# The second feed-forward's output product in seven-product block form, turned, in a written order

## The chip, the cores and the metric

The kernel runs on one core of a Trainium2 chip. Its engines run at the same time, each through its own queue in order: TensorE (PE, with its weight loads PEld), VectorE (DVE), ScalarE (ACT), GpSimd (POOL) and SyncE (SP), which issues nearly all DMAs. The metric is the device time of one execution in microseconds (us). Three runs of the kernel before took 812.83, 813.78 and 814.72 us; the median is 813.78.

## The reference

Three stages, all in float32:

```python
def _attn_ref(q, k, v):                        # q, k, v: 4 batches, 8 heads, 576 rows, 64 columns
    scores = scale * np.matmul(q, k.transpose(0, 1, 3, 2))
    ...                                        # heads 0-3: a local mask, heads 4-7: every 32nd row
    return np.matmul(softmax(scores), v)

def _moe_ref(x, w_gate, w_val, w_out):         # x: 2304 tokens x 512; inner width 1536
    g = x @ w_gate
    silu = g * (1.0 / (1.0 + np.exp(-g)))
    return silu * (x @ w_val) @ w_out

def _moe2_ref(x, w1, w2, w3, w_out):           # inner width 768
    h = np.maximum(np.maximum(x @ w1, x @ w2), x @ w3)
    return h @ w_out                           # 2304 x 512
```

The change concerns the last line, `h @ w_out`.

## The kernel before

Matrix products keep float32 accuracy by splitting each operand into a high part, rounded to the matmul's type, and a low part, the rest. A product is then three matmuls: high x high, high x low, low x high (`product`, L643; `factor_product`, L770). Making the two parts is one ScalarE copy and one subtraction on VectorE or GpSimd (`split`, L169).

**The first half**, up to 530.7 us, does attention and the first feed-forward. The tokens run in five columns ("chunks") of up to 448 tokens; for each chunk and each of 12 slices f of the inner width a slot holds gate, value and output products (`emit_gate`, `emit_val`, `emit_out`). Beside it the weights of the second feed-forward are made ready in the order of the list `later` and stored to DRAM (`pair_steps` L256 for w1 to w3, `wo2_steps` L291 for w_out). The result y, transposed (512 rows x 2304 tokens), is stored to `ydr`. A scheduler orders most of this from estimated times; only the beginning is written out by hand.

**The second half** runs in three passes of 768 tokens, each as two column blocks of `TB` = 384. Its first part, the three products y @ w1, w2, w3, is done in blocks of two by two with seven block products in place of eight (the Strassen-Winograd form). Per pass there are three pairs g of inner slices and in each three matrices i, nine groups, 27 in all. `Group` (L780) computes one: with A for the weight's factors and B for y's, seven products of two row halves x three terms = 6 matmuls of 384 columns each, 42 in all, in three PSUM banks a, b, c. `head` has A11 (B11) into a and A12 (B21) into b; `middle` S2 (T2) into a, S1 (T1) into c, S3 (T3) into a; `tail` A22 (T4) into a and S4 (B22) into c. Between products into bank a ScalarE takes snapshots (`snap`, L787) that VectorE adds in later (`emit`, L795). The maximum over the three matrices is kept in t11, t12, t21, t22; at i = 2 it is split into h's high and low parts. The tail of a group is issued behind the head of the next.

The weights' seven factors, high and low, come in one DMA of 1792 KB per group into a ring of `NRING` = 4 tiles (`load_w`, L763). y's blocks are loaded into raw tiles, the factors T1 to T4 are made from them, and all are split (`load_y` L734, `split_y` L754).

**The output product before** (`mm` L841, `out2` L853): for each block of 128 tokens j, six inner slices x three terms = 18 matmuls with h as the stationary operand and 512 columns of w_out moving, into a bank z; 18 blocks in three passes, 324 matmuls. w_out is loaded once, 3072 KB. The first inner slices of blocks 0 and 1 (`z_early`) are free to move ahead, and the scheduler puts them between groups. Each z is copied to `osb` by VectorE or ScalarE and stored; the last one in two halves, on two queues.

## Time and profile before

| | before |
|---|---|
| median of 3 runs | 813.78 us (812.83 to 814.72) |
| profiled execution | 814.75 us, of which the span is 813.0 us |
| TensorE busy | 795.3 us, 98% of the span, 4588 matmuls |
| VectorE, ScalarE, GpSimd busy | 542.8, 384.2, 235.6 us |
| granted TensorE clock, mean | 0.996 |
| DMA | 200.50 MB, 247 GB/s |
| second half | from 530.70 us |

The span goes from the first to the last instruction on the core; the profiled execution's time is 1.75 us longer. Matmuls overlap in the pipeline and the busy time contains each one's whole latency, so a busy share says how seldom TensorE had nothing, and not at what pace it worked: the pace is the distance between starts.

### The profile page before, as it was taken

How to read it: one execution, taken by the hardware profiler on the slowest of the kernel's cores; microseconds unless marked ns; L12 is line 12 of the kernel's file. 1: busy time of each engine (PE TensorE's matmuls, PEld its weight loads, DVE VectorE, ACT ScalarE, POOL GpSimd, SP SyncE). 2: the span in 40 equal slices, each digit the busy share in tenths (PEclk: the TensorE clock that was granted, in tenths of full speed). 3: DMA queues.
4: the chain of work that ended last, by engine and by line, in shares of the span. 5: the costliest groups of instructions: out<-in, count | busy, mean ns of one | idle time of the engine just before them, and what ended most of it. 6: DMA issues, size and time to landing. Idle time of an engine off the chain costs nothing.

```text
span 813.0 us, 12942 instructions
## 1 busy us (share of the span) xinstructions
PE 795.3 (98%) x4588; PEld 711.5 (88%) x4588; DVE 542.8 (67%) x1104; ACT 384.2 (47%) x856; POOL 235.6 (29%) x237
## 2 busy tenths in 40 slices
PE   6999999999999999999999999999999999999998
PEld 5777777888998998888999999999999989989986
DVE  5899997888969899799993863634454344613440
ACT  6999994455454634555342543423242123512220
POOL 2534442022312432314232664502212121402110
PEclk9899999999999999999999999999999999999999
DMA  9998887777766887757676997789646566634402
GB/s 281 322 326 290 303 311 270 262 242 226 261 235 208 264 285 246 264 208 258 231 262 212 346 392 294 281 342 354 237 181 232 168 210 213 260 148 181 181 1 77
DMA packets 69688, 200.50 MB, mean 247 GB/s; under 512 B 8088, under 2 KB 33432, under 8 KB 66040
## 3 DMA queue, kind: packets, MB, share of 16 engines
q1 hardware_dynamic: 69480, 199.55, 70.0%
q8 instruction: 36, 0.59, 0.3%
q14 instruction: 28, 0.23, 0.1%
q10 hardware_dynamic: 144, 0.13, 0.0%
HBM read 157.97 MB, written 41.68 MB: 246 GB/s over the span
## 4 chain that ended last, share of the span: by engine, by line
PE 55%; DVE 4%; DMA 2%; issue 1%; ACT 1%; SPq 0%; POOL 0%; DVEq 0%; ACTq 0%
PE ps_a L775 13%; PE ps_z L849 9%; PE ps_c L775 7%; PE ps_b L775 3%; PE ps_y L645 3%; PE ps_y L647 3%; PE ps_y L646 3%; PE ps_v L645 3%; PE ps_v L647 3%; PE ps_v L646 2%; PE ps_g L645 2%; PE ps_g L646 2%; PE ps_g L647 2%; DMA wr<-wsdr 1%; DVE pr L552 1%
## 5 line engine op out<-in xcount | busy, mean ns | idle before, releaser
L680 POOL TENSOR_TENSOR hl<-ht,hh 128x448 fp32r<-128x448 f32 x48 | 61.6, 1284 | 228.1 <-ACT hh L676 206.4
L176 POOL TENSOR_TENSOR hl<-t,hh 128x384 fp32r<-128x384 f32 x36 | 37.7, 1050 | 208.0 <-ACT hh L173 160.0
L775 PE MATMUL ps_a<-yhT,wr 128*128 128x384 f32 x324 | 94.6, 339 | 1.1 <-ACT s L789 1.1
L645 PE MATMUL ps_g<-xh,wh_g 128*128 128x448 f32 (+1 forms) x240 | 90.8, 378 | 1.0 <-ACT ht L664 1.0
L645 PE MATMUL ps_v<-xh,w_v 128*128 128x448 f32 (+1 forms) x240 | 91.2, 380 | 0.4 <-DVE ht L671 0.2
L646 PE MATMUL ps_g<-xl,wh_g 128*128 128x448 f32 (+1 forms) x240 | 89.8, 374 | 0.0
L647 PE MATMUL ps_y<-hh,w_o 128*128 128x448 f32 (+1 forms) x240 | 89.4, 373 | 0.3 <-DVE w_o L249 0.3
L647 PE MATMUL ps_g<-xh,wl_g 128*128 128x448 f32 (+1 forms) x240 | 89.5, 373 | 0.0
L646 PE MATMUL ps_y<-hl,w_o 128*128 128x448 f32 (+1 forms) x240 | 89.2, 372 | 0.0
L646 PE MATMUL ps_v<-xl,w_v 128*128 128x448 f32 (+1 forms) x240 | 89.2, 372 | 0.0
L647 PE MATMUL ps_v<-xh,w_v 128*128 128x448 f32 (+1 forms) x240 | 89.1, 371 | 0.0
L789 ACT ACTIVATE s<-ps_a 128x384 f32<-128x384 f32 x81 | 39.4, 490 | 99.0 <-PE ps_a L775 98.7
L676 ACT ACTIVATE hh<-ht 128x448 fp32r<-128x448 f32 (+1 forms) x60 | 35.3, 588 | 104.7 <-DVE ht L671 93.4
L645 PE MATMUL ps_y<-hh,w_o 128*128 128x448 f32 (+1 forms) x240 | 84.3, 380 | 0.0
L849 PE MATMUL ps_z<-wo2t,hh 128*128 128x512 f32 x216 | 64.8, 392 | 0.9 <-ACT osb L867 0.7
L775 PEld LDWEIGHTS ps_a<-yhT,wr 128*128 128x128 f32 x324 | 59.7, 188 | 2.6 <-ACT s L789 2.1
L775 PE MATMUL ps_a<-ylT,wr 128*128 128x384 f32 x162 | 54.8, 338 | 0.0
L645 PEld LDWEIGHTS ps_g<-xh,wh_g 128*128 128x128 f32 x240 | 45.4, 189 | 7.1 <-ACT ht L664 1.8
L645 PEld LDWEIGHTS ps_v<-xh,w_v 128*128 128x128 f32 x240 | 45.1, 188 | 6.5 <-DVE ht L671 1.1
L647 PEld LDWEIGHTS ps_g<-xh,wl_g 128*128 128x128 f32 x240 | 45.3, 189 | 5.4 <-DVE wl_g L249 0.4
L647 PEld LDWEIGHTS ps_y<-hh,w_o 128*128 128x128 f32 x240 | 45.1, 188 | 5.6 <-DVE w_o L249 0.7
L645 PEld LDWEIGHTS ps_y<-hh,w_o 128*128 128x128 f32 x240 | 45.0, 188 | 5.6
(150 smaller groups left out, 1843.2 us busy)
## 6 DMA issues: line engine op xcount, KB each, us to landing
wr<-wsdr SPq DMA_DIRECT2D x27, 1792.0 KB, 7.3
raw<-in_w_dram SPq DMA_DIRECT2D x60, 512.0 KB, 6.0
w_v<-wvdr SPq DMA_DIRECT2D x48, 512.0 KB, 4.5
w_o<-wodr SPq DMA_DIRECT2D x48, 512.0 KB, 4.6
wsdr<-whi SPq DMA_DIRECT2D x27, 256.0 KB, 2.9
wvdr<-w_v SPq DMA_DIRECT2D x12, 512.0 KB, 3.7
wodr<-w_o SPq DMA_DIRECT2D x12, 512.0 KB, 3.9
wsdr<-w SPq DMA_DIRECT2D x18, 256.0 KB, 3.3
```

The costliest lines, as they stand in the source:

```text
L176: return a.ins, lo_eng.tensor_tensor(lo, src, f32(hi), ALU.subtract).ins
L552: eng.tensor_tensor(pv, self.k[:, 0:i + 1, :], self.q[:, r:r + 1, :].to_broadcast([128, i + 1, D]), ALU.mult)
L645: nc.tensor.matmul(ps, wh, xh, start=first, stop=False)
L646: nc.tensor.matmul(ps, wh, xl, start=False, stop=False)
L647: nc.tensor.matmul(ps, wl, xh, start=False, stop=last)
L676: return nc.scalar.activation(hs[c, f][0], t, AF.Copy).ins
L680: return eng.tensor_tensor(hl, t, f32(hh), ALU.subtract).ins
L775: nc.tensor.matmul(ps, wts[:, c, a, ks], y[k][b], start=first and k == q == 0, stop=k == 1 and q == 2, skip_group_check=True,)
L789: nc.scalar.activation(s, self.a, AF.Copy)
L849: nc.tensor.matmul(z[j], a[:, ts], w[:, f, b], start=f == q == 0, stop=f == NF2 - 1 and q == 2)
```

## The change

The output product gets the seven-product form too, and is turned: w_out's factors are the stationary operand (from the same ring, as a fourth matrix i = 3 of each pair g, made by `pair_steps(3, g)`), h's factors move, 384 tokens at a time, and the result is stored transposed; the host turns it back. So h is no longer split block by block: for each pair g the blocks t11 to t22 become factors (`Factors.combine`) and then high and low parts (`Factors.split`), three subtractions on VectorE and one on GpSimd, seven copies on ScalarE, five low parts on VectorE and two on GpSimd (T3, B22). The same class serves y, whose blocks B11, B21, B22 are loaded straight into the tiles that later hold their low parts. The conversion steps wait in a list, `waiting`, and `some(n)` issues the next n of them at written places. `outputs` runs one pass's output: for each half m of 128 rows seven products of 18/2 = 9 matmuls (three pairs x three terms); the parts of A11, A12 and S1 that need only pairs 0 and 1 come first, around the last group's tail. The next y is loaded and converted inside `outputs`. The ring has five tiles; the three weights of an output hold three of them until the pass ends. From the eleventh slot of the last chunk to the end, `manual_schedule` keeps the written order.

The change in the diff, cut to its core:

```diff
-NRING = 4
+NRING = 5
...
+            if i == 3:
+                a12, a21 = a21, a12
...
+        eng = nc.vector if (c, f) == (NC - 1, NF - 1) else nc.gpsimd
+        last_val[:] = [m, high_h(c, f, t), low_h(c, f, t, eng)]
 
...
+    class Factors:
+
+
+        def __init__(self, p, tag):
+            self.p, self.tag, self.parts, self.raw = p, tag, {}, {}
+
+        def part(self, q, f):
+            return self.p.tile([128, TB], F32R, name=f"{self.tag}{q}{f}", tag=f"{self.tag}{q}{f}")
+
+        def fresh(self, f):
+            r = self.raw[f] = r_p.tile([128, TB], F32, name=f"r{f}", tag=f, bufs=3 if f == "T3" else 1)
+            return r
+
+        def combine(self):
+            b12 = self.raw["T3"]
+            nc.vector.tensor_tensor(self.fresh("T1"), b12, self.raw["B11"], ALU.subtract)
+            nc.gpsimd.tensor_tensor(b12, self.raw["B22"], b12, ALU.subtract)
+            nc.vector.tensor_tensor(self.fresh("T2"), self.raw["B22"], self.raw["T1"], ALU.subtract)
+            nc.vector.tensor_tensor(self.fresh("T4"), self.raw["B21"], self.raw["T2"], ALU.subtract)
+
+        def split(self, f):
+            src = self.raw.pop(f)
+            hi, lo = self.part("h", f), self.parts.get(f) or self.part("l", f)
+            self.parts[f] = hi, lo
+            split(hi, lo, src, nc.scalar, nc.gpsimd if f in ("T3", "B22") else nc.vector)
+
+    waiting = []
+
+    def some(n):
+        for _ in range(min(n, len(waiting))):
+            waiting.pop(0)()
+
+    def conversion(fs, names):
+        return [fs.combine] + [lambda f=f: fs.split(f) for f in names]
+
+    def load_y(p):
+        y = [Factors(y_p, f"y{k}") for k in range(2)]
+        for k in range(2):
+            for n in ("B11", "B12", "B22", "B21"):
+                if n == "B12":
+                    r = y[k].fresh("T3")
+                else:
+                    y[k].parts[n] = y[k].part("l", n)
+                    r = y[k].raw[n] = f32(y[k].parts[n])
+                m, t = 2 * int(n[1]) - 2 + k, (2 * PASSES[p] + int(n[2]) - 1) * TB
+                for c, i0, i1, o in pieces(t // STRIDE, (t + TB) // STRIDE):
+                    nc.sync.dma_start(
+                        r[:, o * STRIDE:(o + i1 - i0) * STRIDE], ydr[c][:, m, i0 * STRIDE:i1 * STRIDE]
+                    )
+        for k in range(2):
+            waiting.extend(conversion(y[k], FACTORS[:-1]))
+        waiting.extend(lambda k=k: y[k].split("B22") for k in range(2))
         return y
 
     ring = {}
...
+    def factor_product(ps, pieces, piece, wts, bs, first, last):
+        c = pieces.index(piece)
+        for n, ((w, ks), (bh, bl)) in enumerate(zip(wts, bs)):
+            for q, (a, b) in enumerate(((0, bh), (0, bl), (1, bh))):
                 nc.tensor.matmul(
-                    ps, wts[:, c, a, ks], y[k][b], start=first and k == q == 0, stop=k == 1 and q == 2,
-                    skip_group_check=True,
+                    ps, w[:, c, a, ks], b, start=first and n == q == 0,
+                    stop=last and n == len(wts) - 1 and q == 2, skip_group_check=True,
                 )
+
+    def banks(first=None):
+        ps = (first or m_p, m_p, m_p)
+        return (q.tile([128, 512], F32, name=f"ps_{n}", tag=n)[:, :TB] for q, n in zip(ps, "abc"))
+
+    def snap(ps, n):
+        s = s2_p.tile([128, TB], F32, name=f"s{n}", tag=f"s{n}", bufs=1 + (n < 3))
+        nc.scalar.activation(s, ps, AF.Copy)
+        return s
 
...
-            t = run[blk]
+            t = to = run[blk]
+            if self.i == 2:
+                h2.setdefault(self.g, Factors(h2_p, f"h{self.g}"))
+                to = h2[self.g].fresh("T3") if blk == "12" else t
+                h2[self.g].raw.setdefault("B" + blk, t)
             if s is None:
-                nc.vector.tensor_tensor(t, ps, t, ALU.max)
+                nc.vector.tensor_tensor(to, ps, t, ALU.max)
             else:
                 nc.vector.tensor_tensor(s, ps, s, ALU.add)
-                nc.vector.tensor_tensor(t, s, t, ALU.max)
-            if self.i == 2:
-                f, h = 2 * self.g + int(blk[0]) - 1, int(blk[1]) - 1
-                hh, hl = h2[f]
-                ts = slice(h * TB, (h + 1) * TB)
-                split(hh[:, ts], hl[:, ts], t, nc.scalar, nc.gpsimd)
+                nc.vector.tensor_tensor(to, s, t, ALU.max)
 
...
+        def finish(self):
+            if self.i == 2:
+                waiting.extend(conversion(h2[self.g], FACTORS))
+
     run, h2 = {}, {}
...
+    class Out:
+
+
+        def __init__(self, p, m):
+            self.p, self.m = p, m
+            self.w = [ring[p, g, 3] for g in range(NFP)]
+            self.a, self.b, self.c = banks()
+
+        def mul(self, n, piece, f, gs=range(NFP), last=False):
+            ms = slice(self.m * 128, (self.m + 1) * 128)
+            factor_product(
+                getattr(self, n), OUT_PIECES, piece, [(self.w[g], ms) for g in gs], [h2[g].parts[f] for g in gs],
+                gs[0] == 0 and piece in ("A11", "A12", "S1"), last
+            )
+
+        def snap(self, n):
+            setattr(self, f"s{n}", snap(self.a, n))
+
+        def emit(self, blk, ps, s=None):
+            t0 = (2 * PASSES[self.p] + int(blk[1]) - 1) * TB
+            rows = slice((int(blk[0]) - 1) * 256 + self.m * 128, (int(blk[0]) - 1) * 256 + (self.m + 1) * 128)
+            osb = osb_p.tile([128, TB], F32, name="osb", tag="osb")
+            if s is None:
+                nc.scalar.activation(osb, ps, AF.Copy)
             else:
-                nc.scalar.activation(osb, z[j], AF.Copy)
-            nc.sync.dma_start(out[t0:t0 + 128, :], osb)
-
-        for j in range(2 * TB // 128):
-            mm(j, z_late if j < 2 else range(NF2))
-            done(j)
-        z.clear()
-
+                nc.vector.tensor_tensor(osb, ps, s, ALU.add)
+            nc.sync.dma_start(out[rows, t0:t0 + TB], osb)
+
+    def outputs(p, grp, y):
+        early = range(NFP - 1)
+        final = [NFP - 1]
+        o = [Out(p, m) for m in range(2)]
+        o[0].mul("a", "A11", "B11", early)
+        grp.tail()
+        o[0].mul("b", "A12", "B21", early)
+        o[0].mul("c", "S1", "T1", early)
+        o[1].mul("a", "A11", "B11", early)
+        o[1].mul("b", "A12", "B21", early)
+        o[1].mul("c", "S1", "T1", early)
+        grp.finish()
+        ends = p == NP - 1
+        some(len(waiting))
+        if not ends:
+            y = load_y(p + 1)
+            load_w(*work[len(ring)])
+        for t in o:
+            t.mul("a", "A11", "B11", final)
+            t.snap(1)
+            t.mul("b", "A12", "B21", final, True)
+            t.emit("11", t.b, t.s1)
+        some(4)
+        for t in o:
+            t.mul("a", "S2", "T2")
+            t.snap(2)
+            some(1)
+        for t in o:
+            t.mul("c", "S1", "T1", final)
+            t.mul("a", "S3", "T3")
+            t.snap(3)
+            t.emit("22", t.c, t.s3)
+            some(2)
+        for t in o:
+            some(2)
+            if ends and t is o[1]:
+                t.mul("c", "S4", "B22", last=True)
+                t.emit("12", t.c, t.s2)
+                t.mul("a", "A22", "T4", last=True)
+                t.emit("21", t.a)
+            else:
+                t.mul("a", "A22", "T4", last=True)
+                t.emit("21", t.a)
+                t.mul("c", "S4", "B22", last=True)
+                t.emit("12", t.c, t.s2)
+        for _ in range(NFP):
+            if len(ring) < len(work):
+                load_w(*work[len(ring)])
+        return y
 
     wdr = {(n, f): dram.tile([128, 2, 512], F32, name=f"w{n}dr{f}") for n in "vo" for f in range(NF)}
-    wsdr = {(i, g): dram.tile([128, 7 * 2 * 256], F32, name=f"wsdr{i}{g}") for i in range(3) for g in range(NFP)}
-    wo2dr = dram.tile([128, NF2, 2, 512], F32, name="wo2dr")
+    wsdr = {(i, g): dram.tile([128, 7 * 2 * 256], F32, name=f"wsdr{i}{g}") for i in range(4) for g in range(NFP)}
 
     first = [("g", 0), ("v", 0)]
     for f in range(NF):
@@ -943,12 +1005,16 @@
             for i, st in enumerate(attention_steps(c)):
                 fill.setdefault((c - 1) * NF + i - 3, []).extend(st)
         later = [step for g in range(NFP) for i in range(3) for step in pair_steps(i, g)]
-        later += [step for f in range(NF2) for step in wo2_steps(f)]
+        later += [step for g in range(NFP) for step in pair_steps(3, g)]
         due, done = 0.0, 0
+        seam = ExitStack()
         for s, (c, f) in enumerate(slots):
+            if (c, f) == (NC - 1, SEAM + 1):
+                seam.enter_context(tc.manual_schedule())
             if c > 0:
-                reload("v", f)
-                reload("o", f)
+                if c < NC - 1 or f <= SEAM:
+                    reload("v", f)
+                    reload("o", f)
                 emit_val(c, f, emit_gate(c, f))
             with ExitStack() as tied:
                 if c == 0:
@@ -967,15 +1033,19 @@
                 assert not later
...
+                y = load_y(0)
                 load_w(0, 0, 0)
+            if c == NC - 1:
+                some(len(waiting) if f == NF - 1 else 5)
             if c > 0:
                 emit_out(*pending)
                 pending = c, f
+        seam.close()
         emit_out(*pending)
     one.close()
 
...
-            if (g, i) == (NFP - 1, 2):
-                mm(0, z_early)
-                grp.tail()
-                mm(1, z_early)
-                before = None
-                out2(p)
-                if p + 1 < NP:
-                    y = [split_y(raw[k]) for k in range(2)]
-
+        for p in range(NP):
+            h2.clear()
+            for g in range(NFP):
+                for i in range(3):
+                    grp = Group(p, g, i, y)
+                    grp.head()
+                    some(2)
+                    if before is not None:
+                        before.tail()
+                    grp.middle()
+                    if before is not None:
+                        before.finish()
+                    some(4)
...
+                    before = grp
+            y = outputs(p, grp, y)
+            before = None
 
...
-    return r.results[0]["out_0_dram"]
+    return _np.ascontiguousarray(r.results[0]["out_0_dram"].T)
```

Three places of the order in which the instructions stand. In the names, `y0hB11` is the high part of factor B11 of y's first row half, `h2lT2` the low part of T2 of h's pair 2; `ps_a`, `ps_b`, `ps_c` are the PSUM banks, `wr` a ring tile.

TensorE, last group of the kernel, from its product S3 to its product A22, before:

```order
L775 MATMUL ps_a_8038<-yhT3_7536,wr_7853 128x384
L775 MATMUL ps_a_8038<-ylT3_7537,wr_7853 128x384
L775 MATMUL ps_a_8038<-yhT3_7536,wr_7853 128x384
L775 MATMUL ps_a_8038<-yhT4_7512,wr_7853 128x384
L775 MATMUL ps_a_8038<-ylT4_7513,wr_7853 128x384
L775 MATMUL ps_a_8038<-yhT4_7512,wr_7853 128x384
```

and now:

```order
L790 MATMUL ps_a_8345<-y1hT3_7763,wr_8126 128x384
L790 MATMUL ps_a_8403<-h0hB11_8037,wr_8186 128x384
L790 MATMUL ps_a_8403<-h0lB11_8038,wr_8186 128x384
L790 MATMUL ps_a_8403<-h0hB11_8037,wr_8186 128x384
L790 MATMUL ps_a_8403<-h1hB11_8254,wr_8266 128x384
L790 MATMUL ps_a_8403<-h1lB11_8255,wr_8266 128x384
L790 MATMUL ps_a_8403<-h1hB11_8254,wr_8266 128x384
L790 MATMUL ps_a_8345<-y0hT4_7697,wr_8126 128x384
```

Before, A22 followed S3 on the same bank at once; now the output's first product, of six matmuls into another bank, stands between them.

SyncE's queue, before, where the second pass's y is loaded, in the middle of the first pass (L742 y, L766 weights):

```order
L766 DMA wr_6062<-wsdr21_138 128x3584
L742 DMA rB11_6064<-ydr3_105 128x384
L742 DMA rB12_6066<-ydr4_106 128x384
L742 DMA rB21_6068<-ydr3_105 128x384
L742 DMA rB22_6070<-ydr4_106 128x384
L742 DMA rB11_6079<-ydr3_105 128x384
L742 DMA rB12_6081<-ydr4_106 128x384
L742 DMA rB21_6083<-ydr3_105 128x384
L742 DMA rB22_6085<-ydr4_106 128x384
L766 DMA wr_6156<-wsdr02_133 128x3584
L766 DMA wr_6220<-wsdr12_136 128x3584
```

and now, at the first pass's end (L770 y, L783 weights, L887 results):

```order
L783 DMA wr_6525<-wsdr32_142 128x3584
L783 DMA wr_6585<-wsdr00_131 128x3584
L770 DMA y0lB11_6680<-ydr3_105 128x384
L770 DMA rT3_6682<-ydr4_106 128x384
L770 DMA y0lB22_6684<-ydr4_106 128x384
L770 DMA y0lB21_6686<-ydr3_105 128x384
L770 DMA y1lB11_6688<-ydr3_105 128x384
L770 DMA rT3_6690<-ydr4_106 128x384
L770 DMA y1lB22_6692<-ydr4_106 128x384
L770 DMA y1lB21_6694<-ydr3_105 128x384
L783 DMA wr_6696<-wsdr10_134 128x3584
L887 DMA out_0_dram<-osb_6706 128x384
```

The eight loads of y moved from the first pass's groups to its output, into tiles that the groups read until then, and stand behind the load of the next pass's first weights and ahead of its second and of all results.

VectorE, behind the last group of the kernel, before (the last maxima, then copies of z):

```order
L806 TENSOR_TENSOR t21_8004<-ps_a_8038,t21_8004 128x384
L808 TENSOR_TENSOR s2_8080<-ps_c_8040,s2_8080 128x384
L809 TENSOR_TENSOR t12_8012<-s2_8080,t12_8012 128x384
L865 COPY osb_8160<-ps_z_8132 128x512
L865 COPY osb_8204<-ps_z_8185 128x512
L859 COPY osb_8248<-ps_z_8229 128x256
```

and now:

```order
L832 TENSOR_TENSOR s2_8385<-ps_c_8347,s2_8385 128x384
L833 TENSOR_TENSOR rT3_8428<-s2_8385,t12_8309 128x384
L739 TENSOR_TENSOR rT1_8461<-rT3_8428,t11_8205 128x384
L741 TENSOR_TENSOR rT2_8464<-t22_8245,rT1_8461 128x384
L742 TENSOR_TENSOR rT4_8466<-t21_8301,rT2_8464 128x384
L176 TENSOR_TENSOR h2lB11_8469<-t11_8205,h2hB11_8468 128x384
L176 TENSOR_TENSOR h2lB21_8473<-t21_8301,h2hB21_8472 128x384
L176 TENSOR_TENSOR h2lT2_8477<-rT2_8464,h2hT2_8476 128x384
L176 TENSOR_TENSOR h2lT1_8481<-rT1_8461,h2hT1_8480 128x384
L176 TENSOR_TENSOR h2lT4_8489<-rT4_8466,h2hT4_8488 128x384
L886 TENSOR_TENSOR osb_8504<-ps_b_8404,s1_8499 128x384
```

Behind the last maximum (`rT3`, L833) three combinations and five low parts now stand on VectorE ahead of the first result.

## Rows read from the trace of the kernel before

**Rows 1.** Windows: length, busy us (instructions) by engine, clock, DMA share, GB/s.

```profile
430.00:530.70 100.70, 100.70 (x498) 92.99 (x497) 54.68 (x79) 42.96 (x84) 51.25 (x46) 1.00 0.85 305
530.70:813.00 282.30, 275.87 (x1459) 259.72 (x1458) 114.42 (x195) 80.00 (x165) 50.96 (x48) 1.00 0.54 197
```

**Rows 2.** Windows of TensorE: line 775 (groups), then line 849 (output).

```profile
530.70:813.00 282.30, 206.94 (x1134) 1.00 0.54 197
530.70:813.00 282.30, 81.30 (x324) 1.00 0.54 197
```

**Rows 3.** Chain of waits, pieces in order of time: start us, us, what.

```profile
530.70 1.28 PE ps_a L775 x6
...
552.02 2.12 PE ps_a L775 x12
...
792.72 16.64 PE ps_z L849 x72
```

**Rows 4.** Waits of TensorE, 500 to 813 us: total us, times, longest.

```profile
PE ps_a L775 <- ACT s L789: 1.1, 2, 0.6
PE ps_z L849 <- ACT osb L867: 0.7, 1, 0.7
PE ps_b L775 <- DMA wr<-wsdr: 0.7, 1, 0.7
```

**Rows 5.** Timeline near the end: start us, us, engine, instruction, [idle before, releaser].

```profile
786.50 0.33 PE L775 MATMUL ps_a<-yhT,wr 128*128 128x384 f32 x1
786.93 0.49 ACT L789 ACTIVATE s<-ps_a 128x384 f32<-128x384 f32 x1 [1.95 <-PE ps_a L775]
...
787.47 0.44 PE L775 MATMUL ps_a<-yhT,wr 128*128 128x384 f32 x1 [0.64 <-ACT s L789]
```

**Rows 6.** VectorE by line and shape, 530 to 813 us: count, busy us, mean ns.

```profile
L809 DVE TENSOR_TENSOR t<-s,t 128x384 f32<-128x384 f32 x54 | 36.0, 667 | 1.5
L808 DVE TENSOR_TENSOR s<-ps_c,s 128x384 f32<-128x384 f32 x36 | 20.0, 556 | 41.7 <-ACT s L789 33.2 <-PE ps_c L775 8.4
...
L176 DVE TENSOR_TENSOR ylB<-rB,yhB 128x384 fp32r<-128x384 f32 x12 | 7.5, 630 | 4.1 <-ACT yhB L173 4.1
...
L751 DVE TENSOR_TENSOR rT<-rB,rT 128x384 f32<-128x384 f32 x4 | 3.6, 904 | 0.1
```

**Rows 7.** ScalarE and GpSimd by line and shape, the same stretch.

```profile
L789 ACT ACTIVATE s<-ps_a 128x384 f32<-128x384 f32 x81 | 39.4, 490 | 99.0 <-PE ps_a L775 98.7
L173 ACT ACTIVATE hh<-t 128x384 fp32r<-128x384 f32 x36 | 18.9, 524 | 38.3 <-DVE t L809 27.2 <-DVE t L806 11.0
...
L176 POOL TENSOR_TENSOR hl<-t,hh 128x384 fp32r<-128x384 f32 x36 | 37.7, 1050 | 208.0 <-ACT hh L173 160.0 <-issue 21.5 <-PE ps_a L775 19.3
```

**Rows 8.** Timeline of VectorE and GpSimd while y's factors are made.

```profile
649.93 0.56 DVE L750 TENSOR_TENSOR rT<-rB,rT 128x384 f32<-128x384 f32 x1 [0.59 <-DMA rB<-ydr]
...
650.00 1.36 POOL L748 TENSOR_TENSOR rB<-rB,rB 128x384 f32<-128x384 f32 x1 [1.24 <-DMA rB<-ydr]
...
650.52 1.25 DVE L751 TENSOR_TENSOR rT<-rB,rT 128x384 f32<-128x384 f32 x1
```

**Rows 9.** DMA issues, 500 to 813 us: count, KB each, median us to landing.

```profile
wr<-wsdr SPq DMA_DIRECT2D x26, 1792.0 KB, 7.3
out_dram<-osb SPq DMA_DIRECT2D x17, 256.0 KB, 2.0
...
rB<-ydr SPq DMA_DIRECT2D x12, 192.0 KB, 7.7
...
out_dram<-osb ACTq DMA_DIRECT2D x1, 128.0 KB, 1.8
```

**Rows 10.** Timeline of the end.

```profile
808.96 0.39 PE L849 MATMUL ps_z<-wo2t,hl 128*128 128x512 f32 x1
...
810.25 0.37 ACTq L862 DMA_DIRECT2D out_dram<-osb  x1
```

**Rows 11.** Timeline of TensorE where the second half begins.

```profile
530.34 0.37 PE L647 MATMUL ps_y<-hh,w_o 128*128 128x448 f32 x1
530.68 0.44 PE L775 MATMUL ps_a<-yhB,wr 128*128 128x384 f32 x1
```

More of the change, by code (lines that the diff above doesn't have):

```diff
@@ L784, in __init__ @@
             self.g, self.i, self.w, self.y = g, i, ring[p, g, i], y
[L785 to L790 removed]
+            self.a, self.b, self.c = banks(a_p if (p, g, i) == (0, 0, 0) else m_p)
         def mul(self, ps, piece, f, first, last):
[L793 removed]
+            halves = [(self.w, slice(k * 128, (k + 1) * 128)) for k in range(2)]
+            factor_product(ps, PIECES, piece, halves, [t.parts[f] for t in self.y], first, last)
         def emit(self, blk, ps, s=None):
             if self.i == 0:
[L798 removed]
+                t = run[blk] = t_p.tile([128, TB], F32, name=f"t{blk}", tag=f"t{blk}", bufs=1 + (blk in ("11", "22")))
                 if s is None:
@@ L993, in tile_attention_swiglu_maxout @@
-        wo2 = wo2_p.tile([128, NF2, 2, 512], F32R, name="wo2t")
+        a_p = sub(two, "a", 1, space=PS, reuse_waits="tile")
+        work = []
+        for p in range(NP):
+            work += [(p, g, i) for g in range(NFP) for i in range(3)] + [(p, g, 3) for g in range(NFP)]
         for n in range(1, NRING):
-            last = load_w(*work[n])
-        with tc.issue_after(last):
-            nc.sync.dma_start(f32(wo2), wo2dr)
+            load_w(*work[n])
+        ctx.enter_context(tc.manual_schedule())
```

121 lines of the change are left out of this document (17 added, 104 removed).

## The prediction

> **What bounds the kernel now.** I read four views of the second half, from 530.70 us to the end. First, the windows by stage: TensorE is busy 275.87 of 282.30 us at the full granted clock, VectorE 114.42, ScalarE 80.00, GpSimd 50.96, DMA 0.54 of its engines [rows 1]. Nothing but TensorE is near its limit, and in the last 100 us of the first half the other engines have 46 us or more to spare as well. Second, the same window for the two matmul lines alone gives the counts: 1134 products of 384 columns in the groups, 324 of 512 columns in the output [rows 2]. Third, the chain of waits runs through those products, and its pieces give the pace without the overlap that the busy time contains: twelve of 384 columns take 2.12 us, so 0.1765 us each, and 72 of 512 columns take 16.64 us, so 0.2311 us each [rows 3]. Fourth, the waits of TensorE name what little is lost: 1.1 us for ScalarE's snapshots, 0.7 for an output bank, 0.7 for a weight load [rows 4].
>
> From these the half adds up. 1134 x 0.1765 + 324 x 0.2311 = 200.2 + 74.9 = 275.1 us of work. TensorE's first product starts at 530.70 and its last, at 808.96, ends 0.23 later [rows 3, 10], which is 278.5 us: 3.4 us are idle, of which rows 4 name 2.5 and the pipeline's refill after each stop the rest.
>
> **What the change does, part by part.** *The output product.* 324 products of 512 columns go. Seven products, each two row halves x three pairs x three terms, make 126 per pass and 378 in three passes, all of 384 columns: the group's own shape, with the same one weight load for each. 378 x 0.1765 = 66.7 us against 74.9: **-8.2 us**, all on TensorE, which is the path.
>
> *The old idle time.* The stop of 0.6 us stands where S3 and A22, both into bank a, follow each other: A22 needs the snapshot between them [rows 4, 5]. In the new order a full product stands there at least; the first order piece shows it. The output bank's stop goes because the output has six banks of its own sequence. The weight stop at the start of the second pass goes because the two weights that begin a pass have slots while the output still holds three of five. **-3.4 us**; bounds 0 and -3.4; I take all of it and count what comes in its place.
>
> *Waits that can come.* After a product's last slot ends ScalarE starts 0.25 us later (786.50 + 0.18 to 786.93) and TensorE 0.05 us after ScalarE ends [rows 5]; two VectorE instructions in a row are 0.04 apart (649.93 + 0.56 to 650.52) [rows 8].
> (a) Between S2 and S3 stands S1 alone, 1.06 us, for a chain of 0.25 + 0.49 + 0.05 = 0.79 us [rows 5, 7]. The margin is 0.27 us, 27 times. Bounds 0 and 2.7 (0.1 each); I take 0.2.
> (b) The end of a pass, three times. The last pair's factors start when S4 ends; 30 products of the output that use pairs 0 and 1 cover 30 x 0.1765 = 5.3 us. The chain on VectorE (third order piece) is add 0.56, max 0.67, T1 0.56, T2 0.56, T4, low half of B11 0.63 [rows 6, 8], with 0.25 + 6 x 0.04 + 0.05 of hand-overs. T4 falls beside GpSimd's T3. Row 650.52 has just that pair: T4 took 1.25 us beside GpSimd's 1.36 [rows 8], against 0.904 in the mean [rows 6]. With 1.25 the chain is 4.8 us, without any conflict 4.0, and with B11's low half at 1.25 as well 5.4. Bounds 0 and 0.3 in all; I take 0.
> (c) After pairs 0 and 1, six times. ScalarE's queue has the high half of T2 ahead of the next group's first snapshot, and behind that snapshot stands S2. From the end of S3: 0.25 + 0.49 (snapshot), 0.56 (emit), 0.56 (T1), 0.56 (T2), 0.52 (high half), 0.49 (snapshot) [rows 6 to 8], with hand-overs 3.7 us, against four products of six, 4.24 us. T2 at 1.25 makes it 4.35, T1 too 5.04. Bounds 0 and 4.8 us (6 x 0.8); I take 0.4.
> (d) The next y, twice. Sixteen conversion steps of VectorE now lie inside the output: 2 x (0.56 + 0.56 + 1.25 + 5 x 0.63) = 11.0 us, four emits 2.2, hand-overs 0.8: 14.0 us. They start at 11.4 us after the last group's S3 (48 matmuls 8.5, twelve more 2.1, then 0.25 and the emit's 0.56) and TensorE asks for the second half's T2 at 26.5 (the tail's 12 matmuls, the output's 126, and 12 of the next group): 15.1 us. Two low halves of T3 on GpSimd may block 0.7 us each. Bounds 0 and 0.8; I take 0.2.
> (e) The y loads themselves. They go into tiles that the products just left, so B22's load waits for S4, 3.2 us after S3. A load of 192 KB took 7.7 us to land [rows 9], so 10.9; the first combine comes at 11.4. But the loads queue behind one of 1792 KB (7.3 us, rows 9) that is issued within the last group, and ahead of the next. Behind a late load stands all of VectorE's and ScalarE's queue, so lateness is paid in full. Bounds 0 and 3 (two passes, 1.5); I take 0.1. On SP's queue the results' DMAs stand behind them, as the second order piece shows; the first result exists only at 9.9 us, and there are four buffers for results.
> (f) The seam. The first product of the second half moves ahead of the last two output products of the first, into a bank of its own, and y's conversions stand in a written order among the last three columns. Before, 0.14 us were lost there (530.34 + 0.20 to 530.68) [rows 11]; the first product into a bank of y's accumulators now waits the same way. VectorE is 46 us idle in the 100 before [rows 1]. Bounds -0.2 and 1; I take 0.1.
> New waits taken: 0.2 + 0 + 0.4 + 0.2 + 0.1 + 0.1 = **+1.0 us**; bounds -0.2 and 12.6.
>
> *Weights.* Three loads of 1792 KB more per pass and one of 3072 KB less in all: 9 x 1.835 - 3.1 = 13.4 MB in a stretch whose engines are 0.54 busy [rows 1]; 36 loads of 7.3 us [rows 9] would fit into its 268 us even one behind the other. Preparing the weights adds a few 256-column steps in the first half, under the same cover as (f). I take 0.
>
> *The end.* Before, the last product ends at 809.19 and the span at 813.0, with one half of the last tile after the other and 1.8 us of landing [rows 10]. Now one copy of 0.49 and one DMA of 192 KB, between the 1.8 of 128 KB and the 2.0 of 256 KB [rows 9, 10]: **-0.2 us**; bounds -0.4 and +0.3.
>
> *A rule against it.* The low halves move from GpSimd to VectorE while GpSimd keeps three steps of each conversion. The Trainium skill, "SBUF — State Buffer", "Who interferes with whom", says that a VectorE instruction with two SBUF inputs and a GpSimd instruction that reads SBUF exclude each other for the whole instruction. The trace agrees: T4, issued at 650.52 beside GpSimd's step until 651.36, ends 0.41 us after it. By the rule each of GpSimd's three steps can hold one of VectorE's, also the low halves; the sum would be about 1 us higher, 0.15 from (b) and 0.8 from (d).
>
> **The sum.** Profiled execution 814.75 (span 813.0, 1.75 around it): -8.2 - 3.4 + 1.0 - 0.2 = 803.95. The median shown, 813.78, is 0.97 lower: **803.0 us**.
>
> **Rivals.**
> 1. *The work goes and the idle time stays* (24%): the new order stops as often at other places, 3.4 in place of 1.0. For it: the margins of (a) and (c) are a few tenths. Against: each of the four old stops has its cause removed. 803.0 + 2.4 = 805.4.
> 2. *y arrives late* (8%): the loads share the engines with both neighbours, 5.2 MB, and land some 4 us late, twice: 803.0 + 8 = 811. For it: 7.7 us for so small a load [rows 9]. Against: two ring loads need not be under way when they are issued.
> 3. *VectorE becomes the bound* (3%), the slower side: if all eight steps of each conversion ran at 1.25 us, (b) would be 6.7 - 5.3 = 1.4 us late three times, (c) 0.8 six times, (d) 23.0 - 15.1 = 7.9 twice: 24.8 us, so 803.0 - 0.6 + 24.8 = 827. It decides from 10.8 us of stops beyond those taken, 1 us at each of the eleven places. Against: GpSimd has 3.5 us of steps per conversion (1.36 + 2 x 1.05, rows 7, 8), which cannot hold eight.
> 4. *The shorter products do not run at the group's pace* (3%): at 0.198 us each 378 cost the 74.9 of before, and 811 results. Against: 1134 of the same shape, each with its own weight load, run at 0.1765.
>
> **How the numbers follow.** The forecast has 62%: 801.2 (no stop at all, 802.0, and the spread of the runs) to 804.4. The range reaches through rival 1 and into the blocked ends of (c): 801.2 to 807.5, and leaves out rivals 2 to 4 and a tail of the forecast's own bounds. A change under 0.2% (1.6 us) can't be told from none here. Faster by more: the forecast, rival 1 and most of 2 and 4, 0.93; same 0.03; slower 0.04.
>
> **What would show it.** Matmuls of the new line: 1512, and chain pieces of twelve in 2.12 us, also in the output; TensorE's part from its first group product to its last 268 us, not 278.5. Waits of TensorE on ScalarE's snapshots under 1 us in all; a row of TensorE waiting for VectorE's factors or for y's DMA, at the three pass ends, would speak for rival 1 or 2. T4 near 1.25 beside T3. It is wrong if the output's products are spaced wider than 0.18 us, or if VectorE shows no gaps around the pass ends.

## The result and the profile after

The changed kernel took 800.63 us in the median of five runs (798.39 to 802.30), the kernel before 813.78 (811.62 to 814.72): a ratio of 0.984, 95% interval 0.9813 to 0.9867. The forecast was 803.0, with a range from 801.2 to 807.5; the kernel is 2.4 us faster than that and lies 0.6 under the range. Two more series of the same kernel gave 801.71 and 800.72 us, ratios 0.9861 (0.9847 to 0.9876) and 0.9840 (0.9818 to 0.9862). Of all runs below one was slow, in the kernel with all low parts on GpSimd (1280.53 us at a granted clock of 0.56), and that kernel's median leaves it out.

The profiled execution took 801.86 us, its span is 800.1; before, 814.75 and 813.0. The forecast's sum was 803.95, so the trace is 2.1 us under it. The same views as before, in the same order. First the windows of the second half (length, busy us and instructions by engine, clock, DMA share, GB/s): all engines (PE, PEld, DVE, ACT, POOL) in one, and in the other the line of block products alone (PE, PEld):

```profile
530.00:796.00 266.00, 266.00 (x1513) 265.50 (x1512) 170.99 (x278) 93.42 (x205) 50.89 (x41) 1.00 0.69 258
...
525.60:800.10 274.50, 266.25 (x1512) 265.43 (x1511) 1.00 0.69 259
```

Against [rows 1] VectorE has gone from 114 us to 171, and TensorE is busy without a break. [rows 2] had 1134 + 324 products; now there are 1512 of one shape. The chain of waits through the first pass's end (start us, us, what):

```profile
600.60 1.06 PE ps_a L790 x6
601.67 1.05 PE ps_b L790 x6
602.72 1.05 PE ps_c L790 x6
603.77 0.52 PE ps_a L790 x3
604.29 0.54 PE ps_b L790 x3
604.83 0.52 PE ps_a L790 x3
605.35 0.52 PE ps_b L790 x3
605.87 3.17 PE ps_a L790 x18
...
619.62 1.06 PE ps_a L790 x6
620.68 1.06 PE ps_b L790 x6
```

Each piece begins where the one before ends: the last group, the output and the next pass run into each other at 0.176 us per product, and no other engine is in the chain. TensorE's waits, the whole list of the run (us, times, longest):

```profile
PE ps_a L376 <- DMA raw<-in_st_dram: 6.0, 4, 4.0
PE ps_a L416 <- DVE xl L463: 2.5, 1, 2.5
PE ps_a L376 <- DMA qke<-in_locqk_dram: 1.2, 2, 0.6
PE ps_a L416 <- ACT q L209: 1.0, 1, 1.0
PE ps_g L634 <- ACT ht L653: 1.0, 2, 0.6
PE ps_a L376 <- DVE state L386: 0.3, 1, 0.3
PE ps_y L636 <- DVE w_o L249: 0.3, 1, 0.3
PE ps_v L634 <- DVE ht L660: 0.2, 1, 0.2
```

Line 790, that of the block products, is not among them: the waits of [rows 4] are gone and none has come. What is left stands at the seam (answers to [rows 11]), and the end answers to [rows 10]:

```profile
531.39 0.37 PE L636 MATMUL ps_y<-hh,w_o 128*128 128x448 f32 x1
531.71 0.44 PE L790 MATMUL ps_b<-y0hB,wr 128*128 128x384 f32 x1
532.00 0.34 PE L790 MATMUL ps_b<-y0lB,wr 128*128 128x384 f32 x1
...
796.26 0.33 PE L790 MATMUL ps_a<-h2hT,wr 128*128 128x384 f32 x1
796.63 0.49 ACT L884 ACTIVATE osb<-ps_a 128x384 f32<-128x384 f32 x1 [4.28 <-PE ps_a L790]
797.14 0.33 SPq L887 DMA_DIRECT2D out_dram<-osb  x1
```

**The account.** The distance from the first start of the second half's products to their last is 270.66 us (525.60 to 796.26), of which 24 products of the first half that stand between take 4.95; with 0.18 for the last product that leaves 265.9 us. Before, it was 278.28 + 0.23 = 278.5. So the second half lost 12.6 us; the rest of the 12.9 by which the profiled executions differ lies in the end (3.81 to 3.66 us behind the last product) and in the first half (0.1). "Idle" below is the sum, over all distances between the start of a block or output product and the next start that exceed the mean by 30%, of what they exceed it by: 4.77 us before, 0.11 after. The stop behind the last of the 24 products, 0.12 more, is not in it. The means without these are 0.1760 us (384 columns) and 0.2287 (512) before, 0.1757 after.

### The profile page after: what moved, and what is told of

The parts are those of the page before. It is cut to its first block, busy times and chain, and to the rows that moved or that the text cites. A ratio compares the mean times of both kernels' runs of the same rounds, so it can differ in the third digit from the quotient of the medians.

```text
span 800.1 us, 13307 instructions
## 1 busy us (share of the span) xinstructions
PE 783.8 (98%) x4642; PEld 715.9 (89%) x4642; DVE 614.5 (77%) x1201; ACT 399.8 (50%) x903; POOL 234.9 (29%) x230
## 4 chain that ended last, share of the span: by engine, by line
PE 57%; DVE 4%; issue 1%; ACT 1%; DMA 0%; DVEq 0%
PE ps_a L790 19%; PE ps_c L790 9%; PE ps_b L790 5%; PE ps_y L634 3%; PE ps_y L636 3%; PE ps_y L635 3%; PE ps_v L634 3%; PE ps_v L636 3%; PE ps_v L635 3%; PE ps_g L634 2%; PE ps_g L635 2%; PE ps_g L636 2%; DVE pr L541 1%; DVE pr L563 1%; DVE sto L566 0%
## 5 line engine op out<-in xcount | busy, mean ns | idle before, releaser
L801 ACT ACTIVATE s<-ps_a 128x384 f32<-128x384 f32 x99 | 48.4, 489 | 135.2 <-PE ps_a L790 135.2
L740 POOL TENSOR_TENSOR rT<-t,rT 128x384 f32<-128x384 f32 x9 | 12.5, 1390 | 149.6 <-DVE rT L739 149.6
L790 PE MATMUL ps_a<-y0hT,wr 128*128 128x384 f32 x162 | 54.9, 339 | 0.0
L790 PE MATMUL ps_a<-y1hT,wr 128*128 128x384 f32 x162 | 54.5, 337 | 0.0
L634 PEld LDWEIGHTS ps_v<-xh,w_v 128*128 128x128 f32 x240 | 45.1, 188 | 6.6 <-DVE ht L660 1.1
L635 PEld LDWEIGHTS ps_g<-xl,wh_g 128*128 128x128 f32 x240 | 45.4, 189 | 4.8
L636 PEld LDWEIGHTS ps_v<-xh,w_v 128*128 128x128 f32 x240 | 45.1, 188 | 5.0
```

What stands on the lines that cost most here:

```text
L634: nc.tensor.matmul(ps, wh, xh, start=first, stop=False)
L635: nc.tensor.matmul(ps, wh, xl, start=False, stop=False)
L636: nc.tensor.matmul(ps, wl, xh, start=False, stop=last)
L740: nc.gpsimd.tensor_tensor(b12, self.raw["B22"], b12, ALU.subtract)
L790: nc.tensor.matmul(ps, w[:, c, a, ks], b, start=first and n == q == 0, stop=last and n == len(wts) - 1 and q == 2, skip_group_check=True,)
L801: nc.scalar.activation(s, ps, AF.Copy)
```

## The experiments

All numbers of "distance" and "idle" are worked out from each kernel's trace as above. The first half of every kernel that is made from the changed one does the same work, except in the two with transposes.

**The same kernels again.** No edit.

> The changed kernel once more, beside the kernel before on one chip. Theory A (the forecast's terms were mis-sized; the trace of the changed kernel is 2.1 us under the forecast's sum): the medians differ by 12 to 13.5 us again, a ratio near 0.984. Theory B (the terms were right and the first runs happened to be low): they differ by 10.8 us, a ratio near 0.987. The single runs should spread by some 4 us with the mean granted clock: 0.995 the longest, 1.0 the shortest.

> The changed kernel a third time. If the second half's 270.7 us is fixed and only the start moves, its trace has 270.7 us again, and its median lies between 800 and 802.5 us, 11 to 13 us under the kernel before.

> The kernel before, once more with a profile. Theory A (its idle time in the second half is a property of its order): 278.3 us from the first to the last start of the second half's products again, 4.8 us of them idle, at the same places. Rival (idle time differs from run to run as the start does): off by a microsecond or more.

The changed kernel: medians 801.71 and 800.72 us, 11.1 and 12.9 under the kernel before. Its distance is 270.68 (527.13 to 797.81) and 270.70 us (523.53 to 794.23), so three traces agree to 0.04 us; their starts differ by 3.6. By the medians the second series lies nearer theory B and the third nearer theory A; the traces decide for A, since all three have the same second half. The clock does not order the runs as expected: in the second series the shortest, 801.00 us, had the lowest clock, 0.995. The kernel before: 813.52 us, 277.99 us from first to last start, 4.41 idle: the same places, with the weight stop 0.52 in place of 0.85. The second half is fixed; what moves single runs is the start. Two traces at the first gate product, the changed kernel's second series above, the kernel with 54 products more (next experiment) below:

```profile
28.07 0.48 PE L634 MATMUL ps_g<-xh,wh_g 128*128 128x512 f32 x1
```

```profile
24.07 0.52 PE L634 MATMUL ps_g<-xh,wh_g 128*128 128x512 f32 x1
```

4.0 us apart, after instructions that are the same in both; at the second half they are 4.5 apart (527.13 and 522.66). The changed kernel's third series has this product at 23.41 us.

**The price of an output product.**

```diff
+                t.mul("a", "A22", "T4")
                 t.mul("a", "A22", "T4", last=True)
```

> Every output product A22 x T4 is done twice: 54 products of 384 columns more (6 times 9). Theory A (the output's products lie wholly on the path, at the pace 0.1757 us that the trace of the changed kernel gives): 54 x 0.1757 = 9.5 us more than the changed kernel, 18 in 3.16 us there. Rival 4 of the prediction, at the 512-column products' 0.2287: 12.3 us more. If the output's stretch were bound by the conversions beside it: under 5 us more.

Distance 280.14 us, 9.48 more than the changed kernel: 0.1756 us for each of the 54, idle 0.11 as before. The median, 808.78, is 7 to 8 us higher, with the scatter of the starts in it. The output lies wholly on the path at the group's pace, and rival 4 of the prediction falls. 378 + 54 = 432 products is also what the plain eight-product form takes in this shape.

**The covering product.**

```diff
-        o[0].mul("a", "A11", "B11", early)
         grp.tail()
+        o[0].mul("a", "A11", "B11", early)
```

> One line moved: at the end of each pass the last group's tail stands directly behind its S3 again, and the output's first product behind the tail. Theory A: the stop of before returns, 0.8 us each (0.97 between two starts in place of 0.176), three times: 2.4 us, named as a wait for ScalarE's snapshot at three places. Rival (something else ended it): no stop, 0 us.

Distance 273.14, 2.48 more; 802.91 us. The first of three equal places:

```profile
596.56 0.34 PE L790 MATMUL ps_a<-y1hT,wr 128*128 128x384 f32 x1
597.47 0.44 PE L790 MATMUL ps_a<-y0hT,wr 128*128 128x384 f32 x1 [0.58 <-ACT s L801]
```

0.91 us between two starts: with the refill behind it a wait of 0.58 costs 0.83. That stop of [rows 5] had the cause that the prediction named.

**The cover at the pass's end.** Three VectorE instructions ahead of the last pair's factors:

```diff
+        for _ in range(3):
+            z = h2[NFP - 1].raw["B22"]
+            nc.vector.tensor_tensor(z, z, z, ALU.max)
         grp.finish()
```

> Three more VectorE instructions of 0.56 us (each writes the maximum of a block with itself) stand ahead of the last pair's factors, once per pass: 1.8 us later. In the changed kernel the low part of B21 ends 0.37 us before its product and that of B11 1.1 us. Theory A (the cover of the last pair is that thin, and what is late is paid in full): 1.4 us of stops per pass, 4.2 us in all, at the output's B11 and B21 products. Rival (the chain has more room than the trace's slack shows): under 1 us.

Distance 274.83, 4.17 more, where 4.2 was expected; the median of four runs, 803.05, is only 1.3 to 2.4 higher, since the starts scatter by as much. Two stops per pass, both for low parts:

```profile
603.19 0.44 PE L790 MATMUL ps_a<-h2lB,wr 128*128 128x384 f32 x1 [0.28 <-DVE h2lB L176]
...
604.48 0.45 PE L790 MATMUL ps_b<-h2lB,wr 128*128 128x384 f32 x1 [0.50 <-DVE h2lB L176]
```

That the total came out so close is partly luck: against the output's first product B21's low part ends 1.5 us later and not 1.8, and TensorE's refill behind a stop, 0.1, adds to each pass. The slack itself holds: in the changed kernel that low part ends 0.39, 0.29 and 0.33 us before its product in the three passes, here the product starts 0.06 behind it, and 1.5 - 0.3 gives the 1.2 us by which the product is late. This is the tightest place of the changed kernel that an experiment tried.

**Who makes the factors.** All low parts on GpSimd in one kernel; nothing on GpSimd in the other:

```diff
-            split(hi, lo, src, nc.scalar, nc.gpsimd if f in ("T3", "B22") else nc.vector)
+            split(hi, lo, src, nc.scalar, nc.gpsimd)       # low_pool
+            split(hi, lo, src, nc.scalar, nc.vector)       # no_pool
...
-            nc.gpsimd.tensor_tensor(b12, self.raw["B22"], b12, ALU.subtract)
+            nc.vector.tensor_tensor(b12, self.raw["B22"], b12, ALU.subtract)    # no_pool
```

> All low parts of the conversions on GpSimd, none on VectorE. Theory A (a GpSimd step of this kind costs 1.03 us when VectorE is quiet): 6 to 8 of them per conversion still end before their products, under 1 us of stops. Rival (they cost 1.35 beside VectorE, as in most places of the changed kernel): the next y is 3 to 4 us late, twice, 6 to 8 us in all.

> Nothing of the conversions on GpSimd: its three steps per conversion go to VectorE. Theory A (the exclusion costs as much as the steps): VectorE's steps of 1.26 to 1.37 us beside GpSimd fall to 0.56, the low part of B21 at the pass end is ready 0.6 us earlier than now, VectorE's busy time in the second half stays within 5 us of the changed kernel's, and the time is the same. Rival (VectorE's long steps have another cause): they stay long, VectorE has some 15 us more to do, and the last pair's low parts are late by 0.2 to 1 us per pass.

All on GpSimd: distance 277.22, 6.56 more, 807.92 us. The size is the rival's, the place neither's: TensorE has no wait for a part of y, but for snapshots and for a bank of the output (waits as above); what makes those late was not followed further:

```profile
PE ps_a L790 <- ACT s L801: 2.1, 8, 0.3
PE ps_c L790 <- DVE osb L886: 1.8, 2, 1.0
```

Nothing on GpSimd: distance 270.67, idle 0.11, 802.20 us: the same. The window to set beside the changed kernel's first one above:

```profile
530.00:796.00 266.00, 266.00 (x1513) 265.51 (x1512) 164.09 (x319) 93.00 (x206) 0.00 (x0) 1.00 0.69 258
```

VectorE does 41 instructions more in 6.9 us less, and GpSimd's 50.89 us are gone. The pass's end, changed kernel above, without GpSimd below:

```profile
600.32 0.56 DVE L741 TENSOR_TENSOR rT<-t,rT 128x384 f32<-128x384 f32 x1
600.36 1.39 POOL L740 TENSOR_TENSOR rT<-t,rT 128x384 f32<-128x384 f32 x1 [9.87 <-DVE rT L739]
...
600.91 1.26 DVE L742 TENSOR_TENSOR rT<-t,rT 128x384 f32<-128x384 f32 x1
...
602.09 1.84 DVE L176 TENSOR_TENSOR h2lB<-t,h2hB 128x384 fp32r<-128x384 f32 x2
602.39 1.12 POOL L176 TENSOR_TENSOR h2lT<-rT,h2hT 128x384 fp32r<-128x384 f32 x1 [0.63 <-ACT h2hT L173]
```

```profile
601.78 0.56 DVE L742 TENSOR_TENSOR rT<-t,rT 128x384 f32<-128x384 f32 x1
...
602.26 1.02 DVE L176 TENSOR_TENSOR h2lB<-t,h2hB 128x384 fp32r<-128x384 f32 x2
```

T4 (L742) takes 0.56 in place of 1.26 us, and two low parts 1.02 in place of 1.84: the long instructions were those beside GpSimd. T2 (L741), begun just ahead of GpSimd's step, kept its 0.56; T4, begun while that step ran, ends 0.42 us behind it.

**The y loads.**

```diff
-            y = load_y(p + 1)
             load_w(*work[len(ring)])
+            y = load_y(p + 1)
```

> The loads of the next y stand behind the load of the next pass's second weights (1792 KB) instead of ahead of it, twice. The trace has them 2 to 3 us early now, so they would be 3 to 4 us late. Theory of the prediction (behind a late load stands all of VectorE's and ScalarE's queue, lateness is paid in full): 6 to 8 us more. Rival (the conversions end 3 us or more before their products, which takes up the lateness): 0 to 2 us more.

Distance 271.91, 1.25 more; 801.96 us. In the first of the two places y's blocks land 6.1 to 7.6 us after issue in place of 3.2 to 5.6 (medians by tile). In the changed kernel the last block that the first combination reads lands at 600.63 and the combination starts at 607.00, so this load had 6.4 us to spare, where the prediction saw 0.5. Behind the weights it lands 6.5 us later against the start of the second half, and the combination comes 0.3 us later. The one wait of TensorE that the profile names is 0.7 us for a snapshot, at the second place. So the loads were later than the expected 3 to 4 us, and the spare time took up nearly all of it.

**The order of the second half.** First the changed kernel without its written order there:

```diff
-        ctx.enter_context(tc.manual_schedule())
         before = None
```

> The second half's order is left to the scheduler's estimated times, as in the kernel before; everything else is as in the changed kernel. Theory A (the old idle time went because its causes went: no output bank to wait for, five ring tiles, a product between S3 and A22 can be found): TensorE's waits in the second half stay under 1 us and the time is that of the changed kernel. Rival (the written order is what keeps TensorE fed): 3 to 5 us of stops come back, 803.5 to 805.5 against 800.6.

811.34 us, ratio 0.999 (0.9973 to 1.0007): the whole gain is gone, where the rival expected 3 to 5 us of it. Distance 281.98, idle 11.37. TensorE's waits in the second half:

```profile
PE ps_b L790 <- DMA wr<-wsdr: 2.3, 1, 2.3
PE ps_b L790 <- DVE y0lB L176: 2.3, 1, 2.3
PE ps_c L790 <- DVE osb L886: 1.6, 1, 1.6
PE ps_a L790 <- ACT s L801: 1.4, 2, 1.2
```

The scheduler pulls the next pass's first products in among the output's, by estimated times; its y and weights come later than that, and TensorE's queue stands. Not all of the 11.37 us are idle: after nothing had started on TensorE from 705.97 to 708.57, its granted clock is at the lower level (0.50, 1.2 GHz) from 708.5 to 711.9 us, and ten products there start 0.32 us apart, which costs 1.4 us.

Then the old output product in a written order, twice. The first puts the old program text in order as it stands, with y's eight combinations at one place:

```diff
+        ctx.enter_context(tc.manual_schedule())
...
+            if (g, i) == (1, 1) and p + 1 < NP:
+                for k in range(2):
+                    combine(raw[k])
```

> The kernel before (output product of 324 products of 512 columns, ring of four), with its second half in a written order: head, tail of the group before, middle; the first two output blocks' early slices around the last group's tail; y's factors made at the fifth group and split inside the output. Theory A (form and order add up: the form is worth 7.7 us, the order the 4.8 us of idle time): TensorE's idle time in the second half falls from 4.8 to under 1.5 us and the time by 3.5 to 4.5 us, ratio 0.995. Rival (the written order only pays with the new form; here the output banks, the last snapshot and the weights still stop it): idle 3 us or more, ratio 0.998 or above.

819.37 us, ratio 1.0086 (1.0056 to 1.0115): longer, against the expectation of 3.5 to 4.5 us gained. Idle 11.22 (1.4 of it ten products at the lower clock again, from 668.5 us), waits of TensorE:

```profile
PE ps_a L780 <- ACT s L794: 7.5, 8, 2.1
```

ScalarE, around one of the eight:

```profile
554.95 0.52 ACT L173 ACTIVATE hh<-t 128x384 fp32r<-128x384 f32 x1 [1.54 <-DVE t L814]
...
555.38 0.47 ACT L794 ACTIVATE s<-ps_a 128x384 f32<-128x384 f32 x1
...
555.90 0.44 PE L780 MATMUL ps_a<-yhT,wr 128*128 128x384 f32 x1 [0.51 <-ACT s L794]
```

The snapshot stands behind a copy of h, which waits for VectorE's maximum. The second defers h's conversions and spreads y's combinations:

```diff
-                split(hh[:, ts], hl[:, ts], t, nc.scalar, nc.gpsimd)
+                late.append(lambda: split(hh[:, ts], hl[:, ts], t, nc.scalar, nc.gpsimd))
...
             grp.middle()
             before = grp
+            if (g, i) != (NFP - 1, 2):
+                finish()                     # issues what is in late
+            if g == 1 and i < 2 and p + 1 < NP:
+                combine(raw[i], 0)           # T1, T3
+            if g == 2 and i < 2 and p + 1 < NP:
+                combine(raw[i], 1)           # T2, T4
```

> The kernel before with its second half in a written order once more, now with two things taken from the changed kernel's order: h's copies and low parts are issued behind the middle of the next group, not inside the group that makes the maximum, and y's factors are made in four pieces at four groups. Theory A (the stops of the first written order, 8 waits for ScalarE's snapshots, come from these instructions standing ahead of the snapshots in ScalarE's and VectorE's queues): under 2 us of idle time in the second half, 3 to 4 us less than the kernel before, ratio 0.995 to 0.997. Rival (they come from elsewhere): 5 us or more stay idle.

808.68 us, ratio 0.9948 (0.9927 to 0.9969). Distance 272.98, idle 0.10. With that the two halves of the change stand apart; the second half's idle time and the ratio to the kernel before:

| | scheduler's order | written order |
|---|---|---|
| 324 products of 512 columns | 4.77, 1 | 0.10, 0.995 |
| 378 products of 384 columns | 11.37, 0.999 | 0.11, 0.984 to 0.986 |

(The 11.22 us of the first written order stand outside the table: that an order is written does not make it a good one.) Form alone gains nothing that can be told, order alone 4 us, both together 11 to 13. In the traces the second written order takes 5.3 us off the distance (278.28 to 272.98), and the form 7.3 more (to 265.7 without the 24 products of the first half). The ring of five tiles and the written order at the seam were not tested alone; the second written order has neither and stops no more than the changed kernel.

**The start.** Transposes that nobody reads fill TensorE's idle time before the first gate product:

```diff
+            for _ in range(24):              # 12 in the second kernel, behind VectorE's reading
+                nc.tensor.transpose(self.room[:, 384:], ident, ident)
```

> 24 transposes of the identity, read by nobody, are put on TensorE behind the score products at 18.6 us, into the unused columns of their bank, where it stands idle for 2.5 us and its granted clock falls to 0.5. Theory A (the runs' spread comes from the start: the low clock that follows the idle time costs 16 transposes at 0.23 in place of 0.11 us and six gate products at 0.43 in place of 0.23): the clock stays at 1.0 to 30 us and the time falls by 2 to 3 us, ratio to the kernel before 0.982. Rival (the start is paced by loads and by VectorE and ScalarE, the clock only fills waiting time): the same time as the changed kernel, 0.985.

> The same with 12 transposes that stand behind VectorE's reading of the score bank, so they begin about 1.3 us later and end about when the idle time ends. Theory A: the clock falls later or not at all, and 1 to 3 us are gained. Rival: the same time as the changed kernel, 0.985 of the kernel before.

The changed kernel, then the one with 24 (windows as above):

```profile
20.00:24.00 4.00, 2.04 (x10) 1.98 (x11) 3.60 (x19) 3.39 (x16) 2.56 (x3) 0.62 1.00 394
24.00:28.00 4.00, 4.00 (x16) 3.02 (x14) 1.52 (x3) 3.85 (x7) 1.85 (x3) 0.53 1.05 357
```

```profile
0.00:40.00 40.00, 31.48 (x388) 26.10 (x388) 27.64 (x127) 32.91 (x114) 17.08 (x28) 1.00 0.93 313
```

In the changed kernel TensorE starts nothing from 19.5 to nearly 22 us, and within that stretch the granted clock falls: it is 0.93 from 20.5 to 21.0 us and 0.50, the lower level of 1.2 GHz, from there to 27. With the transposes it does not fall, and the time is the same: 802.03 and 801.18 us, ratios 0.9851 (0.9824 to 0.9878) and 0.9845 (0.9818 to 0.9872). So the low clock is not shown to cost anything; what sets the start, among loads and VectorE, stays open. (The kernel with 12 stops 0.9 us at the seam, behind VectorE's copy `ysb`, so its distance is 271.46; the one with 24 has 270.66.)

None of these kernels beats the changed one.

## Why the prediction was wrong

The direction, the path and most causes were right; the sum came out 2.1 us too high and the range too narrow. Step by step:

- **The old idle time, taken as -3.4 with that as its bound, was -4.8: the step that failed.** The chain's piece of 72 products in 16.64 us [rows 3] ends at the last product's end, so it holds that product's whole latency (0.39 in place of 0.23) and a refill of 0.11 at its start. Read as a pace it gave 0.2311; the mean of starts is 0.2287, and an undisturbed piece of the first pass (the row below the list) has 36 in 8.18, 0.2272. With 0.1765 for 0.1760 as well, 324 x 0.0024 + 1134 x 0.0005 = 1.3 us of idle time were booked as work. The stops that made it up were there to be read: 0.66 at 656.40, 0.85 at 660.37, 0.80 at 786.50, and 1.8 between 789.52 and 792.72. With the refills behind the others that is 4.8, of which [rows 4] name 2.5. All of it went, as forecast; before_written2 shows that the order takes it away by itself.
- **New waits, taken as +1.0, are +0.2**, all at the seam (f: 0.1 taken); this is the second of the mis-sized terms. (a), (c) and (d) are 0. In (d) the last low part of T2 ends at 618.10, and its product starts at 622.29: 4.2 us to spare. In (b) the conclusion held, but B21's low part was the nearest (0.3 to 0.4 us), not B11's (1.1), since it stands beside GpSimd and takes 1.37. In (e) the cover was 6.4 us, not 0.5, so that even a load of 1792 KB ahead of y costs 1.25 us in all: the first combination waits for its turn on VectorE and not for the load.
- **The output product, -8.2, was -7.7**: 324 x 0.2287 = 74.1 against 378 x 0.1757 = 66.4. The mechanism stood; the old pace was too high. Against the old form in a written order (324 x 0.2274 = 73.7) it is 7.3. The groups' own products run 0.0003 us faster than before, 0.3 us in all, which was not in the sum.
- **The end**, -0.2, was -0.15.

The chain's piece of the kernel before that gives the pace without a stop at its end:

```profile
619.66 8.18 PE ps_z L849 x36
```

One of its stops, 1.03 us between two starts, of which the profile names 0.69 as a wait:

```profile
660.37 0.34 PE L775 MATMUL ps_a<-yhT,wr 128*128 128x384 f32 x1
661.40 0.41 PE L775 MATMUL ps_b<-yhB,wr 128*128 128x384 f32 x1 [0.69 <-DMA wr<-wsdr]
```

So -7.7 - 0.3 - 4.8 + 0.2 = -12.6 in the second half, where the forecast had -10.6.

One of the prediction's signs of being wrong appeared, and the step that it was to catch was right: VectorE shows no gap at the first two pass ends (at the first it is busy 20.69 of 21.11 us, from 598.54 to 619.65). TensorE waits for nothing there all the same, since each part is ready before its product; gaps on VectorE are no measure of that, the slack of each part is.

**From the trace to the median.** The forecast took 0.97 us off; the profiled execution lies 1.23 over the median. More important, the low end allowed 0.8 us for the spread of runs, from three runs that spanned 1.9. Five span 3.9, and the starts of ten traces of the changed kernel and its variants with the same first half span 4.5 us (522.66 to 527.16). A range of these few runs was no bound on that: the three medians of the changed kernel are 800.63, 800.72 and 801.71, two below the range and one in it.

**Rivals.** The first fails for the changed kernel, which has 0.2 us of new stops and not 3.4; what it feared comes under the scheduler's order, with 11.4 us. The second has no ground: the loads had 6.4 us to spare. The third had all eight of VectorE's steps in a conversion at 1.25 us; in the trace 35 of 104 are long, 2.7 of eight, and without GpSimd's steps VectorE's part is shorter, not longer. The rule of "SBUF — State Buffer", "Who interferes with whom" in the Trainium skill, that such instructions of the two engines exclude each other, agrees with these traces (0.56 alone, 1.25 to 1.38 when begun while a step of GpSimd ran); the 1 us that the prediction worked out from it did not come, since it fell into slack.

## What to carry to other kernels

A chain's piece gives a pace only where the next piece continues it; where it ends at a stop, subtract the last instruction's latency and the refill, or take the mean of the starts, before what is left over is called idle. A form with fewer products is worth its saving only if the instructions that feed it are placed so that no engine's queue holds a late one ahead of one that TensorE waits for; try the order alone before the form gets the credit. Slack per operand, its end against the start of the product that reads it, tells what a delay costs: here the delay that really reached the operand, less its slack, gave the lateness of the product to a tenth of a microsecond.

## What the runs showed of the hardware

VectorE and GpSimd hold each other up, and the one that begins second is the longer. Of VectorE's 128x384 subtractions in the changed kernel's second half all 26 that were running when a step of GpSimd began took 0.54 to 0.56 us, as they do alone; all 35 that began while a step of GpSimd ran took 1.25 to 1.38 and ended 0.41 to 0.42 behind it. GpSimd took 1.0 alone and up to 1.40 when it began beside VectorE. So giving VectorE the 41 instructions of GpSimd cut its own busy time from 171.0 to 164.1 us. A wait of 0.58 us costs TensorE 0.83. And the first gate product, with the same instructions ahead of it in all ten traces, came anywhere from 23.4 to 28.1 us, in three traces of the changed kernel alone at 23.41, 25.24 and 28.07; what sets it was not found.
